# Attention with a relative bias, then a leaky-ReLU feed-forward: which banks the spare in-pieces take, how batch 0's v is split, and where the fifth pair's rows are copied

## The chip, the cores and the metric

The kernel runs on one core of a Trainium2 chip. The metric is the device time of one execution in microseconds. Five engines work side by side and meet at semaphores: TensorE (PE; its weight loads are shown apart as PEld), VectorE (DVE), ScalarE (ACT), GpSimd (POOL, which here mostly issues loads) and SyncE (SP, which issues stores and transposing DMAs). Matrix products are written to PSUM, in banks of 128 x 512 float32; a bank can be written again only when the engine that reads it is done.

## The reference, cut to what matters

```python
# q, k, v: (8, 8, 576, 64); bias_table: (32, 8); w_in: (512, 2048); w_out: (2048, 512)
scores = matmul(q, k.T) / sqrt(64) + bias_table[bucket(|i - j|)]   # per batch and head
attn = exp(scores - max) / sum(exp(scores - max))
x = matmul(attn, v)                     # to (4608, 512): 8 heads x 64 beside each other
h = x @ w_in
out = maximum(0.01 * h, h) @ w_out      # (4608, 512) float32
```

The bias depends on the distance alone and is constant from distance 128 on, so the kernel multiplies the exponentials by a band of factors near the diagonal and leaves the constant out, which the division cancels.

## The kernel before, in words

**Pairs.** Work goes by pairs of heads: 8 batches with 4 pairs each, n = 0 to 31. A sequence of 576 is cut into four chunks of 128 (NJ = 4) and a tail of 64. For a pair, the rows of q and k are copied beside each other (`pair_rows`, L263, two DVE copies), turned (`transpose_q`, `transpose_k`, L295 and L300; by PE and the m banks up to pair 8, by DMA after that) and multiplied. `score(n, u)` is one part of the scores and its exponential on ACT: u = 0 to 3 are the four key chunks against the first 512 queries (`ps_s`, two buffers of two banks, L320, exponential L333), u = 4 is the last 64 queries against the four chunks (written to the banks o0 and o1, one for each head, L313, exponential in two halves L336), u = 5 is the 64 tail keys (L323 and L324, in a `ps_s` buffer, exponential L340). `band(n, u)` multiplies an exponential by its band factors on DVE (L356).

**Value product.** `av_tails(n)` (L369) multiplies the 64 tail keys with the tails of v, for both heads, and `av(n, e)` (L380) the four chunks for head e; each head has its bank, o0 or o1. DVE then divides (reciprocal L383, product L384) into `opair`, which is transposed into xT by PE (L402, L403) or by DMA (L395).

**Feed-forward.** Rows of xT are taken in groups of 512. An in-piece (`ffn_in`, L428) is four products of 512 columns with w_in into one bank, followed by the leaky ReLU (`leaky`: ACT's Prelu at L439, or DVE at L436 and L437). An out-piece (`ffn_out`, L453) is four products with w_out; four of them fill one bank, which DVE copies out (L471). Both use the two m banks in turn (`bank`), unless `spare` names o0 or o1.

**The order** is written out by hand, engine by engine, in the code's order. From pair 5 on each pair has, in PE's order: scores 0 and 1, the tail products of the pair before, its value product for head 0, a slot with at most one in-piece, the product for head 1, a second slot, scores 2 to 4, then `moe_block` with score 5 inside it. `groups_of` shares out how many pieces a pair gets. If no out-piece is ready, the block does up to four in-pieces: the first two on m banks, the third on o0, the fourth on o1, the last two of them after score 5. Otherwise it does four out-pieces. At the end `moe(2, 0)` or `moe(2)` adds up to two in-pieces; in the first form the first of them sits on o0. The third in-piece of a block occurs in pairs 5, 6, 10, 11, 15 and 20, a fourth in pairs 10, 11, 15 and 20; a single piece at the end after four out-pieces in pairs 9, 13, 14, 17, 18 and 19, two in pairs 21 to 31. After pair 31, `moe_rest` does what is left of the feed-forward.

**The first four pairs** have no feed-forward beside them and an order of their own (L642 to L681). In the last of them, n = 3, `pair_rows(4)` comes first, so that in DVE's order its copies stand before bands 5 and 4 of pair 2, and `transpose_k(4)` comes before score 2.

**Loads** are issued by POOL in order. Batch 0: q and k of heads 0 and 1, 2 and 3, 4 and 5; v of heads 0 and 1, one load each; the two tails of these two heads; q and k of heads 6 and 7; then v of heads 2 to 7 in four chunks and the two tails of these six heads. Then come batch 1 and the weights. POOL issues a load only when the eighth load before it has landed.

Of the kernel before, what the change touches and what calls it, by code (L numbers as in the profile page):

```python
# [37 lines left out]
def kernel(  # L38
# [10 lines left out]
    nc = tc.nc  # L49

    B, H, S, D = q.shape
# [4 lines left out]
    P = 128  # L56
    n_pairs = H // 2
    NJ = S // P
    SL = S - NJ * P
# [34 lines left out]
    NBUF = 2  # L94
# [4 lines left out]
    vn = [per.tile([P, NJ, H, D + 1], BF16, name=f"vn{i}") for i in range(NBUF)]  # L99
    v4 = [per.tile([P, n_pairs, D + 1], BF16, name=f"v4_{i}") for i in range(NBUF)]  # L100
# [13 lines left out]
                in_=src[b, h0:h1, :, :].rearrange("h (r c) d -> r h (c d)", c=NC),  # L114
            )

    def load_v_part(b, chunks, tail):
        i = b % NBUF
        for c in chunks:
            nc.gpsimd.dma_start(  # L120
                out=vn[i][:, c, :, 0:D],
                in_=v[b, :, c * P : (c + 1) * P, :].rearrange("h s d -> s h d"),
            )
        if tail:
            for e in range(2):
                nc.gpsimd.dma_start(
                    out=v4[i][e * SL : (e + 1) * SL, :, 0:D],
                    in_=v[b, e::2, NJ * P : S, :].rearrange("h s d -> s h d"),
                )

    def load_v(b, h0, h1, by_head):
        i = b % NBUF
        p0, p1 = h0 // 2, h1 // 2
        if by_head:
            for h in range(h0, h1):
                nc.gpsimd.dma_start(
                    out=vn[i][:, :, h, 0:D],
                    in_=v[b, h, 0 : NJ * P, :].rearrange("(c s) d -> s c d", s=P),
                )
        else:  # L140
            for c in range(NJ):
                nc.gpsimd.dma_start(  # L142
                    out=vn[i][:, c, h0:h1, 0:D],
                    in_=v[b, h0:h1, c * P : (c + 1) * P, :].rearrange("h s d -> s h d"),
                )
        for e in range(2):
            nc.gpsimd.dma_start(
                out=v4[i][e * SL : (e + 1) * SL, p0:p1, 0:D],
                in_=v[b, h0 + e : h1 : 2, NJ * P : S, :].rearrange("h s d -> s h d"),
            )  # L150

    def clear_v(eng, i):
# [41 lines left out]
    for j, (u, lo, w, m) in enumerate(groups):  # L194
        copy = nc.scalar.copy if j % 3 == 2 else nc.vector.tensor_copy
        copy(out=ub[:, C0 + lo : C0 + lo + m * w].rearrange("h (m w) -> h m w", w=w),
             in_=e8[:, u : u + m].unsqueeze(2).to_broadcast([H, m, w]))
    row = ub[:, :]
    nc.vector.tensor_copy(
        out=ub[:, C0 - BAND + 1 : C0],  # L200
# [33 lines left out]
    load_qk(0, 2, 4)  # L234
    load_qk(0, 4, 6)
    clear_edges(nc.vector, 1)
    load_v(0, 0, 2, True)
    load_qk(0, 6, H)
    load_v(0, 2, H, False)
    clear_v(nc.gpsimd, 1)  # L240
    load_qk(1, 0, H // 2)
    load_qk(1, H // 2, H)
# [20 lines left out]
    def pair_rows(n):  # L263

        b, p = items[n]
        t = prs[n] = pr_pool.tile([RQ, 2, NC, 2 * D], BF16, name="pr")
        for j, src in enumerate((qn, kn)):
            nc.vector.tensor_copy(out=t[:, j, :, :].rearrange("r c (e d) -> r c e d", e=2),
                                  in_=src[b % NBUF][0:RQ, 2 * p : 2 * p + 2, :, :].rearrange("r e c d -> r c e d"))
# [25 lines left out]
    def transpose_q(n):  # L295
        qt = qts[n] = qt_pool.tile([P, S], BF16, name="qt")
        copy = nc.scalar.copy if n <= n_pairs else nc.vector.tensor_copy
        copy(out=qt[:, 0:S].rearrange("p (r c) -> p r c", c=NC), in_=turned_pair(n, 0))  # L298

    def transpose_k(n):  # L300
        kt = kts[n] = kts_[n % 2]
        nc.vector.tensor_copy(out=kt[:, 0:S].rearrange("p (r c) -> p r c", c=NC), in_=turned_pair(n, 1))  # L302
        apart(kt)
# [38 lines left out]
    def band(n, u):  # L342
        b, p = items[n]
        at, at4 = at_view(n), at4_[n % 2]
        hp = hk[:, 2 * p : 2 * p + 2, :]
        if u == 0:
            o, m = at[:, :, 0, 0 : 2 * P], mirrored(hp, P, 3 * P)
        elif u in (1, 2):
            o, m = at[:, :, u, (u - 1) * P : (u + 2) * P], mirrored(hp, 0, 3 * P)
        elif u == NJ:  # L350
            o, m = at[:, :, 3, 2 * P : S], mirrored(hp, 0, S - 2 * P)
        elif u == NJ + 1:
            o, m = at4[:, 3 * P : S], mirrored(hk4[:, p, :], 0, P + SL)
        else:
            return
        nc.vector.tensor_tensor(out=o, in0=o, in1=m, op=ALU.mult)  # L356
# [62 lines left out]
    def ffn_in(T, f, spare=None):  # L419
        if f == 0:  # L420
            gts[T] = gt_pool.tile([P, n_fc, TT], BF16, name="gt")
        t0 = T * TT
        if spare is None:
            pm = bank("pm1")
        else:
            pm = ps_o_pool.tile([P, 512], FP32, name="pm1", tag=f"o{spare}")
        for c in range(n_cc):
            nc.tensor.matmul(pm, lhsT=w_in_sb[:, c, f * P : (f + 1) * P], rhs=xT[c][:, t0 : t0 + TT],  # L428
                             start=(c == 0), stop=(c == n_cc - 1))
        return pm  # L430

    def leaky(T, f, pm, by_vector=False):
        g = gts[T][:, f, :]
        if by_vector:
            low = low_pool.tile([P, TT], BF16, name="low")
            nc.vector.tensor_scalar(low, pm, 0.01, None, op0=ALU.mult)  # L436
            nc.vector.tensor_tensor(out=g, in0=low, in1=pm, op=ALU.max)  # L437
        else:
            nc.scalar.activation(g, pm, AF.Prelu, bias=0.0, scale=1.0, alpha=0.01)  # L439
# [72 lines left out]
    def moe(n_pieces, spare=None):  # L512
        for _ in range(n_pieces):
            if room["left"] > 0 and can("in"):
                piece_in(spare)
                spare = None
                room["left"] -= 1
# [26 lines left out]
    def moe_block():  # L544

        done = 0
        while not can("out") and can("in") and done < 4 and room["left"] > 0:
            T, f = step("in")
            leaky(T, f, ffn_in(T, f, done - 2 if done > 1 else None), done == 1)
            room["left"] -= 1  # L550
            done += 1
            if done < 3:
                yield
        while done < 2:
            done += 1
            yield
        if can("out") and room["left"] >= 4:
            for part in range(4):
                piece_out()
                room["left"] -= 1  # L560
                if part == 1:
                    yield
            moe(2, 0)
        else:
            yield
            moe(2)
        yield
# [30 lines left out]
    def loads(n):  # L598

        b, p = items[n]  # L600
        if n == 0:
            load_w_in(0)
            load_v(1, 0, H, False)
            load_w_in(1)
            load_w_out(0)
        elif n == 2:
            load_qk(2, 0, H // 2)
            load_w_out(1)
        if b < 1 or p < 1 or b > B - 2:
            return  # L610
        nc.gpsimd.tensor_copy(out=tick, in_=ops_[n - 2][0:1, 0, 0:1])  # L611
        if p == 1:
            load_qk(b + 1, H // 2, H)
            load_v_part(b + 1, (0,), False)
        elif p == 2:
            load_v_part(b + 1, (1, 2, 3), False)
        else:
            load_v_part(b + 1, (), True)
            if b + 2 < B:
                load_qk(b + 2, 0, H // 2)  # L620

    def begin(n):
        loads(n)
        if n_pairs < n + 1 < N and not by_dma(n + 1):
            pair_rows(n + 1)
        for m in range(n + 2, min(n + AHEAD + 1, N)):
            if by_dma(m) and m - (AHEAD if m > 2 * n_pairs + 2 else 2) == n:
                pair_rows(m)
                turn_by_dma(m)

    def score(n, u):
        exp(n, u, qk_mm(n, u))
# [7 lines left out]
    score(0, 0)  # L640
    score(0, 1)
    for n in range(n_pairs):  # L642
        begin(n)
        if n == n_pairs - 1:
            pair_rows(n + 1)
        if n > 1:
            band(n - 1, 5)
            band(n - 1, 4)
        if n == 1:
            for u in (0, 1, 2, 5, 4):  # L650
                band(0, u)
        if n == 0:
            score(n, 2)
        transpose_k(n + 1)
        if n < 2:
            spin(3)
        if n > 0:
            score(n, 2)
        if n == 1:
            score(n, 3)  # L660
        if n > 0:
            av_tails(n - 1)
            av(n - 1, 0)
            band(n, 0)
        if n != 1:
            score(n, 3)
        if n > 0:
            av(n - 1, 1)
        transpose_q(n + 1)
        if n < 1:  # L670
            spin(3)
        score(n, 5)
        if n > 0:
            band(n, 1)
            x_transposes(n - 1)
            band(n, 2)
        if n < n_pairs - 2:
            pair_rows(n + 2)
        score(n, 4)
        score(n + 1, 0)  # L680
        score(n + 1, 1)  # L681
# [106 lines left out]
```

## Time and profile before

| | before |
|---|---|
| median of 3 runs (lowest, highest) | 388.04 us (386.69, 388.61) |
| profiled execution | 389.03 us |
| its span, first to last instruction | 387.2 us |
| PE busy | 368.6 us (95%) |
| ACT busy | 241.9 us (62%) |
| DVE busy | 205.0 us (53%) |
| POOL busy | 76.5 us (20%) |
| mean granted TensorE clock | 0.996 |

The profile is of one execution. Busy time is the time in which an engine has an instruction under way; matrix products are pipelined and their ends are modelled. In the rows of the timeline the columns are: start, duration, engine, line, operation, what it writes and reads, how many instructions are merged, and in brackets the idle time of the engine ahead of it with what ended it. In the table of waits they are: who waited for what, the sum in us, how many times, the longest. A row of a window gives its length and for PE, PEld, DVE, ACT and POOL the busy time, then the granted TensorE clock, the share of the DMA engines and GB/s. Times are us from the start of the span.

### The profile page before, as it was taken

The numbers are of one execution on the slowest core, as the hardware profiler recorded it, in microseconds if no ns is written. First come the engines' busy times: TensorE is split into PE (matmuls) and PEld (weight loads), VectorE is DVE, ScalarE is ACT, GpSimd is POOL, SyncE is SP. The second block draws the span as 40 slices with busy tenths as digits, with TensorE's granted clock in tenths as the row PEclk, the third lists the DMA queues.
The fourth block names the chain that finished last, engine by engine and source line by source line (L and its number), as shares of the span: only waits on it lengthen the run. The fifth ranks groups of instructions, "written<-read, shape, count | busy, mean of one in ns | idle before, by whom it ended". The sixth has DMA issues, their size and how long they took to land.

```text
span 387.2 us, 8539 instructions
## 1 busy us (share of the span) xinstructions
PE 368.6 (95%) x3501; PEld 187.3 (48%) x3501; DVE 205.0 (53%) x520; ACT 241.9 (62%) x376; POOL 76.5 (20%) x118
## 2 busy tenths in 40 slices
PE   7878988999999999999999999999999999999996
PEld 3445554555444444544455555555555544444442
DVE  5778577776666666666665666655554300110221
ACT  4979678476857768777687777777777546045000
POOL 8764320223023303330323032100000000000000
PEclk9989999999999999999999999999999999999999
DMA  9999999899849983998699859933211100110122
GB/s 106 180 204 184 207 187 120 99 182 126 109 63 163 126 134 54 162 115 133 106 116 105 130 90 132 129 73 71 40 44 46 46 27 0 56 54 0 59 80 81
DMA packets 104351, 40.05 MB, mean 103 GB/s; under 512 B 83184, under 2 KB 98808, under 8 KB 104312
## 3 DMA queue, kind: packets, MB, share of 16 engines
q0 software_dynamic: 53696, 18.36, 46.0%
q1 hardware_dynamic: 50472, 21.02, 27.1%
q8 instruction: 27, 0.44, 0.5%
q10 hardware_dynamic: 144, 0.13, 0.1%
q14 instruction: 12, 0.10, 0.1%
HBM read 37.68 MB, written 9.45 MB: 122 GB/s over the span
## 4 chain that ended last, share of the span: by engine, by line
PE 80%; DVE 6%; ACT 5%; DMA 4%; POOL 3%; issue 1%; DVEq 0%; POOLq 0%
PE pm L453 31%; PE pm L428 28%; PE ps_o L380 9%; PE ps_s L320 6%; ACT at L333 3%; DMA v<-in_v_dram 2%; ACT gt L439 2%; DVE at L356 2%; DMA xT<-opair 2%; DVE opair L384 2%; PE ps_o L369 2%; PE ps_s L323 1%; DVE qt L298 1%; POOL vn L142 1%; PE ps_tx L402 1%
## 5 line engine op out<-in xcount | busy, mean ns | idle before, releaser
L428 PE MATMUL pm<-xT,w_in_sb 128*128 128x512 bf16 x576 | 138.2, 379 | 5.0 <-ACT at L336 4.6
L439 ACT ACTIVATE gt<-pm 128x512 bf16<-128x512 f32 x138 | 82.7, 599 | 92.5 <-PE pm L428 91.9
L453 PE MATMUL pm<-w_out_sb,gt 128*128 128x512 bf16 x576 | 132.5, 379 | 0.0
L333 ACT ACTIVATE at<-ps_s 128x1024 bf16<-128x1024 f32 x128 | 124.7, 1028 | 8.9 <-PE ps_s L320 8.9
L356 DVE TENSOR_TENSOR at<-at,hk 128x768 bf16<-128x768 bf16 (+3 forms) x160 | 71.4, 453 | 31.5 <-ACT at L336 20.8
L453 PEld LDWEIGHTS <-gt 128*128 128x128 bf16 x576 | 53.0, 98 | 60.6
L428 PEld LDWEIGHTS <-w_in_sb 128*128 128x128 bf16 x576 | 52.4, 98 | 59.4 <-issue 5.4
L471 DVE COPY y<-pm 128x512 f32<-128x512 f32 x33 | 22.8, 691 | 76.7 <-PE pm L453 76.7
L380 PE MATMUL ps_o<-vn,at 128*128 128x65 bf16 x1280 | 50.4, 195 | 0.0
L380 PEld LDWEIGHTS <-at 128*128 128x128 bf16 x1280 | 45.3, 98 | 9.3 <-issue 1.4
L320 PE MATMUL ps_s<-qt,kt 64*128 64x512 bf16 x256 | 40.2, 383 | 1.9 <-ACT at L333 1.4
L383 DVE RECIPROCAL rcp<-ps_o 128x5 f32<-128x5 f32 x64 | 12.3, 192 | 53.4 <-PE ps_o L380 53.4
L611 POOL COPY tick<-opair 1x1 bf16<-1x1 bf16 x18 | 4.6, 255 | 156.6 <-DVE opair L384 156.6
L384 DVE TENSOR_TENSOR opair<-ps_o,rcp 128x320 bf16<-128x320 f32 x64 | 31.5, 492 | 3.3
L120 POOL DMA_DIRECT2D vn<-in_v_dram x24 | 22.8, 956 | 2.6 <-issue 1.1
L340 ACT ACTIVATE at<-ps_s 128x576 bf16<-128x576 f32 x32 | 21.9, 685 | 1.2 <-PE ps_s L324 1.2
L336 ACT ACTIVATE at<-ps_q 128x256 bf16<-128x256 f32 x64 | 21.6, 405 | 0.4 <-PE ps_q L313 0.3
L320 PEld LDWEIGHTS <-kt 64*128 64x128 bf16 x256 | 8.2, 94 | 27.7 <-issue 20.7
L463 ACT COPY y<-pm 128x256 f32<-128x256 f32 x1 | 0.4, 372 | 27.5 <-DVE y L463 27.5
L369 PEld LDWEIGHTS <-at 64*128 64x128 bf16 x320 | 9.4, 94 | 12.3 <-issue 5.7
L302 DVE COPY kt<-tu 128x576 bf16<-128x576 bf16 x23 | 15.3, 664 | 0.0
L298 DVE COPY qt<-tu 128x576 bf16<-128x576 bf16 x23 | 15.0, 650 | 0.0
(57 smaller groups left out, 195.3 us busy)
## 6 DMA issues: line engine op xcount, KB each, us to landing
out_dram<-y SPq DMA_DIRECT2D x35, 256.0 KB, 2.3
qn<-in_q_dram POOLq DMA_DIRECT2D x14, 288.0 KB, 5.0
kn<-in_k_dram POOLq DMA_DIRECT2D x14, 288.0 KB, 6.1
vn<-in_v_dram POOLq DMA_DIRECT2D x28, 128.0 KB, 5.7
w_in_sb<-in_moe_w_in_dram POOLq DMA_DIRECT2D x2, 1024.0 KB, 12.8
w_out_sb<-in_moe_w_out_dram POOLq DMA_DIRECT2D x2, 1024.0 KB, 16.0
qn<-in_q_dram POOLq DMA_DIRECT2D x4, 144.0 KB, 4.1
kn<-in_k_dram POOLq DMA_DIRECT2D x4, 144.0 KB, 4.2
```

Source lines behind the costliest of these rows:

```text
L120: nc.gpsimd.dma_start(out=vn[i][:, c, :, 0:D], in_=v[b, :, c * P : (c + 1) * P, :].rearrange("h s d -> s h d"),)
L320: nc.tensor.matmul(ps[:, e, :], lhsT=kt[r, u * P : (u + 1) * P], rhs=qt[r, 0:512], start=True, stop=True)
L333: nc.scalar.activation(at[:, :, u, 0:512], ps, AF.Exp, scale=scale)
L336: nc.scalar.activation(at[:, e, :, 512:S], ps[e][:, 0 : NJ * SL].rearrange("p (c i) -> p c i", i=SL), AF.Exp, scale=scale)
L340: nc.scalar.activation(at4[:, 0:S], ps.rearrange("p e i -> p (e i)")[:, 0:S], AF.Exp, scale=scale)
L356: nc.vector.tensor_tensor(out=o, in0=o, in1=m, op=ALU.mult)
L380: nc.tensor.matmul(ps[:, ic, :], lhsT=at[:, o : o + P], rhs=vn[b % NBUF][:, c, 2 * p + e, :], start=False, stop=(ic == NJ and c == NJ - 1))
L384: nc.vector.tensor_tensor(out=opair[:, :, e * D : (e + 1) * D], in0=ps[:, :, 0:D], in1=rcp.to_broadcast([P, NJ + 1, D]), op=ALU.mult)
L428: nc.tensor.matmul(pm, lhsT=w_in_sb[:, c, f * P : (f + 1) * P], rhs=xT[c][:, t0 : t0 + TT], start=(c == 0), stop=(c == n_cc - 1))
L439: nc.scalar.activation(g, pm, AF.Prelu, bias=0.0, scale=1.0, alpha=0.01)
L453: nc.tensor.matmul(pm, lhsT=gt[:, f, ts * P : (ts + 1) * P], rhs=w_out_sb[:, f, :], start=(f == 0), stop=(f == n_fc - 1))
L471: nc.vector.tensor_copy(out=y, in_=pm)
```

## The change

Three things are changed.

1. Of the in-pieces that follow score 5 in a block, only the fourth keeps its bank of the value product (o1); the third takes the next m bank. At a pair's end after out-pieces the first piece sits on o0 only if more than one piece is left to do.
2. Batch 0's v: the tails of all eight heads are loaded where those of heads 0 and 1 were; heads 2 and 3 are then loaded by head, and heads 4 to 7 by chunk. The other batches' loads are the same, by functions that are cut in another way.
3. In the fourth pair (n = 3) the rows of the fifth are copied after the first value product of pair 2 and a band, `transpose_k(4)` moves behind the second value product, and score 5 moves ahead of both transposes.

```diff
-    def load_v_part(b, chunks, tail):
...
-    def load_v(b, h0, h1, by_head):
...
+    def load_v_part(b, chunks, h0=0, h1=H):
         for c in chunks:
             nc.gpsimd.dma_start(
+                out=vn[b % NBUF][:, c, h0:h1, 0:D],
+                in_=v[b, h0:h1, c * P : (c + 1) * P, :].rearrange("h s d -> s h d"),
             )
+    def load_v_head(b, h):
+        nc.gpsimd.dma_start(
+            out=vn[b % NBUF][:, :, h, 0:D],
+            in_=v[b, h, 0 : NJ * P, :].rearrange("(c s) d -> s c d", s=P),
+        )
+    def load_v_tail(b):
         for e in range(2):
             nc.gpsimd.dma_start(
+                out=v4[b % NBUF][e * SL : (e + 1) * SL, :, 0:D],
+                in_=v[b, e::2, NJ * P : S, :].rearrange("h s d -> s h d"),
             )
...
-    load_v(0, 0, 2, True)
+    load_v_head(0, 0)
+    load_v_head(0, 1)
+    load_v_tail(0)
     load_qk(0, 6, H)
-    load_v(0, 2, H, False)
+    load_v_head(0, 2)
+    load_v_head(0, 3)
+    load_v_part(0, range(NJ), 4, H)
...
-            leaky(T, f, ffn_in(T, f, done - 2 if done > 1 else None), done == 1)
+            leaky(T, f, ffn_in(T, f, 1 if done == 3 else None), done == 1)
...
-            moe(2, 0)
+            moe(2, 0 if room["left"] > 1 else None)
...
     for n in range(n_pairs):
+        last = n == n_pairs - 1
         begin(n)
-        if n == n_pairs - 1:
-            pair_rows(n + 1)
...
-        transpose_k(n + 1)
+        if not last:
+            transpose_k(n + 1)
...
             av_tails(n - 1)
             av(n - 1, 0)
             band(n, 0)
+        if last:
+            pair_rows(n + 1)
         if n != 1:
             score(n, 3)
         if n > 0:
             av(n - 1, 1)
+        if last:
+            score(n, 5)
+            transpose_k(n + 1)
         transpose_q(n + 1)
         if n < 1:
             spin(3)
-        score(n, 5)
+        if not last:
+            score(n, 5)
```

More of the change, by code (lines that the diff above doesn't have):

```diff
@@ L115, in load_qk @@
             )
-    def load_v_part(b, chunks, tail):
-        i = b % NBUF
+    def load_v_part(b, chunks, h0=0, h1=H):
         for c in chunks:
             nc.gpsimd.dma_start(
-                out=vn[i][:, c, :, 0:D],
-                in_=v[b, :, c * P : (c + 1) * P, :].rearrange("h s d -> s h d"),
-            )
[L124 to L129, printed above, removed]
-    def load_v(b, h0, h1, by_head):
[L132 to L145, printed above, removed]
+                out=vn[b % NBUF][:, c, h0:h1, 0:D],
+                in_=v[b, h0:h1, c * P : (c + 1) * P, :].rearrange("h s d -> s h d"),
+            )
+    def load_v_head(b, h):
[4 more added lines that the diff above has]
+    def load_v_tail(b):
         for e in range(2):
             nc.gpsimd.dma_start(
-                out=v4[i][e * SL : (e + 1) * SL, p0:p1, 0:D],
-                in_=v[b, h0 + e : h1 : 2, NJ * P : S, :].rearrange("h s d -> s h d"),
+                out=v4[b % NBUF][e * SL : (e + 1) * SL, :, 0:D],
+                in_=v[b, e::2, NJ * P : S, :].rearrange("h s d -> s h d"),
             )
@@ L602, in loads @@
             load_w_in(0)
-            load_v(1, 0, H, False)
+            load_v_part(1, range(NJ))
+            load_v_tail(1)
             load_w_in(1)
@@ L613, in loads @@
             load_qk(b + 1, H // 2, H)
-            load_v_part(b + 1, (0,), False)
+            load_v_part(b + 1, (0,))
         elif p == 2:
-            load_v_part(b + 1, (1, 2, 3), False)
+            load_v_part(b + 1, (1, 2, 3))
         else:
-            load_v_part(b + 1, (), True)
+            load_v_tail(b + 1)
             if b + 2 < B:
```

## The prediction

> **What bounds the kernel now.** I read the page first (span, clock line, costliest groups), then the waits of PE, then the timeline around each long wait. The page:
>
> ```profile
> span 387.2 us, 8539 instructions
> PE 368.6 (95%) x3501; PEld 187.3 (48%) x3501; DVE 205.0 (53%) x520; ACT 241.9 (62%) x376; POOL 76.5 (20%) x118
> PE 80%; DVE 6%; ACT 5%; DMA 4%; POOL 3%; issue 1%; DVEq 0%; POOLq 0%
> ```
>
> TensorE is busy 95% of the span and carries 80% of the chain, so a wait of PE that goes shortens the span, unless PE soon meets another wait. The time to be had is the 387.2 - 368.6 = 18.6 us that PE idles. The waits of PE (whole span; the last row: weight loads from 36 to 200 us) show where:
>
> ```profile
> PE pm L428 <- ACT at L336: 4.6, 6, 0.8
> PE ps_o L369 <- DMA v<-in_v_dram: 0.8, 1, 0.8
> ...
> PEld L369 <- issue: 3.9, 9, 0.4
> ```
>
> The first row is the third in-piece of a block, which sits on bank o0 and waits for the exponential of part 4 to read that bank; the second is the tail of v; the last is the first tail product of a pair, nine times. The three edits aim at these rows.
>
> **The change part by part.** The order of instructions on each engine is the same but for the fifth pair's rows, transposes and copies, and batch 0's v loads; no instruction is added or dropped, and SP's queue is unchanged. Which bank a piece writes is not an instruction: it changes waits only. By the code's rules the third in-piece occurs in pairs 5, 6, 10, 11, 15, 20 (six, as the first row has), and a lone piece at a pair's end in pairs 9, 13, 14, 17, 18, 19.
>
> *Third in-piece, four-piece blocks (pairs 10, 11, 15, 20).* Timeline of PE and of ACT in pair 10:
>
> ```profile
> 96.92 0.19 PE L324 MATMUL ps_s<-qt,kt 128*128 128x64 bf16 x1
> 97.88 2.75 PE L428 MATMUL pm<-xT,w_in_sb 128*128 128x512 bf16 x12 [0.77 <-ACT at L336]
> 100.56 0.60 PE L320 MATMUL ps_s<-qt,kt 64*128 64x512 bf16 x4
> 101.01 0.31 PE L369 MATMUL ps_o<-v,at 64*128 64x65 bf16 x10
> ...
> 96.04 0.60 ACT L439 ACTIVATE gt<-pm 128x512 bf16<-128x512 f32 x1
> 97.44 0.67 ACT L336 ACTIVATE at<-ps_q 128x256 bf16<-128x256 f32 x2
> ```
>
> On an m bank the third piece takes the buffer of the first piece of the block, which ACT left at 96.04 + 0.60 = 96.64, so it starts when PE is free, about 97.0. A piece takes about 0.87 us (three in 97.88 to 100.5), so it ends at 97.85. The fourth piece stays on o1, which the second half of L336 leaves at 97.44 + 0.67 = 98.11; it starts at 98.17 instead of 97.88 + 0.87 = 98.75. Gain 0.58 a pair, not 0.77: 0.3 us of wait stays on o1. Four pairs: 2.3 us. In pair 11, where the fourth piece is the last, the next tail product still waits for o1, as now.
>
> *Pairs 5 and 6 (third piece alone).* Pair 5:
>
> ```profile
> 51.04 0.19 PE L324 MATMUL ps_s<-qt,kt 128*128 128x64 bf16 x1
> 52.00 1.02 PE L428 MATMUL pm<-xT,w_in_sb 128*128 128x512 bf16 x4 [0.77 <-ACT at L336]
> 52.95 0.61 PE L320 MATMUL ps_s<-qt,kt 64*128 64x512 bf16 x4
> 53.71 0.33 PE L369 MATMUL ps_o<-v,at 64*128 64x65 bf16 x10
> ...
> 52.08 0.69 ACT L340 ACTIVATE at<-ps_s 128x576 bf16<-128x576 f32 x1
> 53.06 0.60 ACT L439 ACTIVATE gt<-pm 128x512 bf16<-128x512 f32 x1 [0.29 <-PE pm L428]
> ```
>
> The piece would end at 51.95. Next late is the second score of the next pair: its bank is free when L340 ends, at 52.77. So it starts at 52.83, and the tail products at 53.05 instead of 53.71; they no longer wait for the Prelu that reads o0 until 53.66. Gain 0.66 each, 1.3 us.
>
> *Lone piece at the end (six pairs).* Pair 9 into 10, PE, then ACT and DVE:
>
> ```profile
> 90.25 0.60 PE L320 MATMUL ps_s<-qt,kt 64*128 64x512 bf16 x4
> 91.01 0.33 PE L369 MATMUL ps_o<-v,at 64*128 64x65 bf16 x10
> 91.88 1.03 PE L428 MATMUL pm<-xT,w_in_sb 128*128 128x512 bf16 x4
> ...
> 90.36 0.60 ACT L439 ACTIVATE gt<-pm 128x512 bf16<-128x512 f32 x1 [1.80 <-PE pm L428]
> ...
> 89.50 0.69 DVE L471 COPY y<-pm 128x512 f32<-128x512 f32 x1 [0.65 <-PE pm L453]
> ```
>
> From the scores to the tail products there are 0.76 us here and 0.45 in pair 10 (100.56 to 101.01), where no piece holds o0: 0.31 us lost to the Prelu that ends at 90.96. On m it goes: 6 x 0.31 = 1.9 us. The price is an added wait: the next slot's piece (91.88) now takes the buffer of the output piece, which the copy L471 leaves at 90.19. It would come at 91.57, so 1.4 us of cover remain; cost nothing, and behind it would stand the rest of PE's pair.
>
> These three sum to 2.3 + 1.3 + 1.9 = 5.5 us; I take 5.4, since pair 11's last wait may grow by 0.1. Bounds: 1.9 (only the Prelu waits go), and 6 x 0.77 + 8 x 0.31 = 7.1 (every wait goes whole).
>
> *Batch 0's v.* The whole tail goes out ahead of q and k of heads 6 and 7, and heads 2 and 3 ahead of the rest. PE and ACT in the third pair, POOL's queue, and PE, DVE, ACT, POOL and the granted clock by stretches of 3.4 us:
>
> ```profile
> 21.85 0.56 PE L369 MATMUL ps_o<-v,at 64*128 64x65 bf16 x10 [0.84 <-DMA v<-in_v_dram]
> 24.04 1.02 ACT L333 ACTIVATE at<-ps_s 128x1024 bf16<-128x1024 f32 x1 [1.67 <-PE ps_s L320]
> 25.79 0.64 ACT L298 COPY qt<-ps_t 128x576 bf16<-128x576 bf16 x1 [0.72 <-PE ps_t L284]
> 18.66 0.67 POOL L112 DMA_DIRECT2D kn<-in_k_dram  x1 [0.67 <-DMA vn<-in_v_dram]
> 19.20:22.60 3.40, 1.60 (x28) 0.93 (x27) 2.51 (x8) 3.17 (x5) 1.41 (x3) 1.00 1.44 192
> 22.60:26.00 3.40, 3.40 (x48) 2.52 (x44) 1.73 (x6) 1.23 (x2) 3.40 (x5) 0.50 1.29 207
> 26.00:29.40 3.40, 2.46 (x47) 1.50 (x46) 3.32 (x8) 3.40 (x7) 1.59 (x3) 1.00 1.13 213
> ```
>
> Ten loads before, ten after, the same bytes. By the shapes in the code a head is 64 KB, both of its pair's tails 16 KB, a chunk of six heads 96 KB. Up to the second chunk, for whose landing POOL waited until 18.66, 128 + 16 + 192 = 336 KB of v were issued; in the changed order 128 + 64 + 128 = 320 KB hold all that the second pair needs. So it is there before 21.85 - 0.84 = 21.01, where PE began to wait. The larger tails move q and k of heads 6 and 7 by 48 KB, half a chunk; DVE first uses them for the fourth pair. With the stall the half clock behind it goes, if nothing else brings it (a rival, below). ACT gets back 1.67 + 0.72 = 2.4 us; it then runs without a gap and sets the pace. I take 2.2 (bounds 0.8, the DMA wait alone, and 2.4).
>
> *Fifth pair's rows.* DVE, PE, and ACT in the fourth pair:
>
> ```profile
> 27.36 0.35 DVE L268 COPY pr<-qn 96x768 bf16<-96x768 bf16 x1
> 27.63 0.57 DVE L268 COPY pr<-kn 96x768 bf16<-96x768 bf16 x1
> 28.73 0.76 DVE L302 COPY kt<-ps_t 128x576 bf16<-128x576 bf16 x1
> 29.52 0.23 DVE L290 TENSOR_TENSOR kt<-kt,own 128x128 bf16<-128x128 bf16 x1
> 33.63 0.65 DVE L356 TENSOR_TENSOR at<-at,hk 128x192 bf16<-128x192 bf16 x2
> 28.26 0.43 PE L284 MATMUL ps_t<-ident,pr 96*128 96x96 bf16 x6 [0.83 <-DVE pr L268]
> 29.10 0.78 PE L380 MATMUL ps_o<-vn,at 128*128 128x65 bf16 x20
> 33.93 0.24 PE L369 MATMUL ps_o<-v,at 64*128 64x65 bf16 x4 [0.47 <-DVE at L356]
> 27.40 3.87 ACT L333 ACTIVATE at<-ps_s 128x1024 bf16<-128x1024 f32 x4
> ```
>
> Today rows, kt copy and mask fill DVE from 27.36 to 29.75, before the pair's first division. Moved behind that division and a band, they put 0.57 + 0.76 + 0.23 = 1.6 us (the two row copies overlap) into a stretch in which DVE hardly idles, up to the bands of 33.63 that PE awaits at 33.93. In return the first division comes only 0.2 earlier: PE's 0.83 wait for the rows goes, but the third score then waits for a bank until the first exponential ends, 27.40 + 3.87 / 4 = 28.4. The 0.2, and about as much by which each copy starts before the one ahead has quite ended, come off: cost 1.2 (bounds 0 and 1.6). Behind the bands stand the rest of pair 3's products, its transposes and the first in-pieces. The first scores of pair 4 need kt too, which now comes after the second division, so ACT may idle some tenths before them; that lies inside the 1.2, since the products wait longer.
>
> Sum: 5.4 + 2.2 - 1.2 = 6.4 us off. The profiled execution took 389.03 us (387.2 of span and 1.8 around it), the median of the runs is 388.04; I count from 388.5, between them: **382.1 us**.
>
> **The rivals.**
> *The half clock comes back.* The clock is 0.50 from 22.60 to 26.00, after 3.4 us in which PE was busy 1.60; after 2.46 busy it stayed at 1.00. In the changed fourth pair PE idles some 1.3 us until the first exponential frees a bank, and idles twice shortly before, so a stretch of 3.4 us can again be about half busy. Then both value products of pair 2 run slow; one took
>
> ```profile
> 22.34 1.12 PE L380 MATMUL ps_o<-vn,at 128*128 128x65 bf16 x20
> ```
>
> against 0.78 at 29.10: 2 x 0.34 and, with the scores between, about 0.9 us given back: 383.0 us. The Trainium skill, TensorE: Matmul & The Clock Gate, Part 1, says that a free-running window of about 3.4 us with too little PE activity halves the clock; the 3.4 us of 0.50 here agree. By that rule the window's place in each run decides.
>
> *The rows cost more than v gives.* If v brings only its DMA wait of 0.8 and the rows cost 1.6 with 0.4 of ACT behind kt, the early part loses 1.2: 388.5 - 5.4 + 1.2 = 384.3 us.
> *The third piece's wait only moves.* If the fourth piece on o1, or L340's bank, takes back all the 0.77, eight Prelu waits remain as gain: 388.5 - 8 x 0.31 - 1.0 = 385.0 us. The end of L336 speaks against it (0.67 for both halves).
> *Slower.* At the six lone pieces the next slot now waits for the output copy L471. Suppose that copy comes behind the next pair's first division: the product for it ends near 91.88 - 0.31 = 91.57; with the division estimated at the copy's own length, 0.69 each, the buffer is free at 92.95, 1.4 us late, and DVE's rows in between (0.35 + 0.57) make it 2.3: 6 x 2.3 = 13.8, 395.9 us. It decides from 1.4 us a pair (8.3 / 6, to 390.4). The row at 89.50 speaks against it: the copy starts there as soon as the output piece is done.
>
> **How the numbers follow.** Forecast 0.49 (its own range 380.8 to 383.5), half clock 0.23, rows 0.09, moved wait 0.11, slower 0.08. About 0.5% (1.9 us: 386.1 to 390.0) is what a measurement of this kernel can tell from no change. Faster: 0.49 + 0.23 + 0.09 and 0.07 of the moved wait = 0.88; within: 0.04 of it and 0.02 of the last = 0.06; slower 0.06. The range 380.3 to 385.4 takes in the first three and half the fourth; below it lie only both best bounds.
>
> **What would show it.** Right: the wait of L428 for L336 falls from 4.6 to about 1.2 (four times 0.3); the L369 issue waits fall from nine to about one; no wait for v near 21; the fourth pair's bands and the tail products behind them later relative to its start. Wrong: L428 waiting for a DVE copy or a Prelu in the slots, 0.50 clock between 25 and 30 us, or pair 4 starting no earlier than now.

## The result, and the profile after

The changed kernel took 383.54 us (median of 6 runs, 382.98 to 384.84) against 387.28 us for the kernel before (median of 6, 386.69 to 388.61): 0.990 of the time, 95% interval 0.988 to 0.992. The profiled execution took 383.14 us, with a span of 381.4.

From the page of the changed kernel (its line numbers are lower: L428 became L417, L380 became L369, L369 became L358):

```profile
span 381.4 us, 8484 instructions
PE 363.4 (95%) x3447; PEld 186.9 (49%) x3501; DVE 205.0 (54%) x520; ACT 240.7 (63%) x376; POOL 76.0 (20%) x118
PE 83%; DVE 7%; ACT 6%; issue 2%; another core or an unknown queue 1%; DVEq 0%; ACTq 0%
L417 PE MATMUL pm<-xT,w_in_sb 128*128 128x512 bf16 x544 | 136.5, 379 | 2.6 <-ACT at L325 0.7
```

TensorE is still the bound. The waits of PE over the whole span:

```profile
PE ps_s L309 <- ACT at L322: 2.7, 3, 1.2
...
PE ps_s L309 <- ACT at L329: 1.0, 3, 0.4
...
PE pm L417 <- ACT at L325: 0.7, 4, 0.2
PE ps_o L358 <- DVE at L345: 0.4, 1, 0.4
```

The wait of the third piece for the exponential of part 4 was 4.6 us in six waits; 0.7 in four is left, on the fourth piece. The DMA wait for v is gone. At the top now are scores that wait for an exponential: 2.7 us where it was 1.4, of which 1.23 are one wait in the fourth pair.

PE in pairs 5, 9 and 10 of the changed kernel:

```profile
51.22 1.03 PE L417 MATMUL pm<-xT,w_in_sb 128*128 128x512 bf16 x4
52.97 0.39 PE L309 MATMUL ps_s<-qt,kt 64*128 64x512 bf16 x2 [0.40 <-ACT at L329]
53.19 0.33 PE L358 MATMUL ps_o<-v,at 64*128 64x65 bf16 x10
...
89.06 0.61 PE L309 MATMUL ps_s<-qt,kt 64*128 64x512 bf16 x4
89.50 0.32 PE L358 MATMUL ps_o<-v,at 64*128 64x65 bf16 x10
...
95.43 1.03 PE L417 MATMUL pm<-xT,w_in_sb 128*128 128x512 bf16 x4
96.64 1.89 PE L417 MATMUL pm<-xT,w_in_sb 128*128 128x512 bf16 x8 [0.18 <-ACT at L325]
```

In pair 5 the piece starts behind score 5, and the second score then waits 0.40 for L329 (before L340). In pair 9 the tail products follow 0.44 behind the scores, where it was 0.76. In pair 10 the fourth piece waits 0.18 for the second half of the exponential.

To see where the time goes, take the start of the part-4 scores of each pair (L313 before, L302 after) and subtract the first trace of the kernel before. Each column is one trace, in us; pairs are numbered from 0, so that pair 2 is the third and pair 3 the fourth. The last three columns are runs told of below.

| pair | before, us | changed | banks alone | v and banks | before, the trace at full clock |
|---|---|---|---|---|---|
| 1 | 18.64 | -0.05 | 0.05 | 0.07 | 0.26 |
| 2 | 26.42 | -2.12 | 0.57 | -2.11 | -1.83 |
| 3 | 32.12 | -1.09 | 0.61 | -2.30 | -1.97 |
| 4 | 38.67 | 0.16 | 0.84 | -2.33 | -1.99 |
| 6 | 58.20 | -0.51 | 0.17 | -2.99 | -1.98 |
| 12 | 115.90 | -2.69 | -2.01 | -5.17 | -2.00 |
| 13 | 124.48 | -3.06 | -2.38 | -5.54 | -1.97 |
| 21 | 200.46 | -5.86 | -5.18 | -8.33 | -1.97 |
| 31 | 299.70 | -5.86 | -5.18 | -8.33 | -1.97 |

The changed kernel gains 2.12 us up to pair 2, gives back 1.03 by pair 3 and 1.25 by pair 4, and then gains 6.0 us up to pair 21; nothing changes after that. PE and DVE in its third to fifth pair, and two stretches of 3.4 us:

```profile
21.04 0.32 PE L358 MATMUL ps_o<-v,at 64*128 64x65 bf16 x10
26.31 0.39 PE L309 MATMUL ps_s<-qt,kt 64*128 64x512 bf16 x2 [1.23 <-ACT at L322]
28.57 0.35 DVE L257 COPY pr<-qn 96x768 bf16<-96x768 bf16 x1
29.25 0.68 PE L273 MATMUL ps_t<-ident,pr 96*128 96x96 bf16 x12 [0.40 <-DVE pr L257]
30.66 0.44 PE L391 MATMUL ps_tx<-ident,opair 128*128 128x128 bf16 x5 [0.73 <-ACT qt L287]
32.51 0.65 DVE L345 TENSOR_TENSOR at<-at,hk 128x192 bf16<-128x192 bf16 x2
32.82 0.29 PE L358 MATMUL ps_o<-v,at 64*128 64x65 bf16 x4 [0.45 <-DVE at L345]
33.05 1.28 PE L369 MATMUL ps_o<-vn,at 128*128 128x65 bf16 x20
29.40:32.80 3.40, 2.06 (x35) 1.28 (x33) 3.37 (x10) 2.22 (x5) 0.56 (x1) 0.98 2.15 161
32.80:36.20 3.40, 3.38 (x48) 2.58 (x48) 1.13 (x4) 2.13 (x3) 1.70 (x3) 0.52 1.75 179
```

The tail products no longer wait for v. The last bands begin 1.1 us earlier than in the first trace (32.51 against 33.63), not 2.1. Then, from about 32.7 to 36.1, the clock is halved: the value product takes 1.28 instead of 0.78. All that v had given in this trace is gone by pair 4.

### The profile page after: what moved, and what is told of

Its sections match the earlier page's. It is cut to its first block, busy times and chain, and to the rows that moved or that the text cites. A ratio compares the mean times of both kernels' runs of the same rounds, so it can differ in the third digit from the quotient of the medians.

```text
span 381.4 us, 8484 instructions
## 1 busy us (share of the span) xinstructions
PE 363.4 (95%) x3447; PEld 186.9 (49%) x3501; DVE 205.0 (54%) x520; ACT 240.7 (63%) x376; POOL 76.0 (20%) x118
## 4 chain that ended last, share of the span: by engine, by line
PE 83%; DVE 7%; ACT 6%; issue 2%; another core or an unknown queue 1%; DVEq 0%; ACTq 0%
PE pm L442 32%; PE pm L417 28%; PE ps_o L369 10%; PE ps_s L309 7%; ACT at L322 4%; DVE at L345 2%; DVE opair L373 2%; PE ps_w L579 1%; PE ps_o L358 1%; PE ps_s L312 1%; ACT at L325 1%; PE ps_tx L391 1%; DVE qt L287 1%; DVE pr L257 1%
## 5 line engine op out<-in xcount | busy, mean ns | idle before, releaser
L417 PE MATMUL pm<-xT,w_in_sb 128*128 128x512 bf16 x544 | 136.5, 379 | 2.6 <-ACT at L325 0.7
L428 ACT ACTIVATE gt<-pm 128x512 bf16<-128x512 f32 x138 | 83.0, 602 | 88.1 <-PE pm L417 86.9
L442 PE MATMUL pm<-w_out_sb,gt 128*128 128x512 bf16 x555 | 130.8, 379 | 1.1
L417 PEld LDWEIGHTS <-w_in_sb 128*128 128x128 bf16 x576 | 52.1, 98 | 55.5 <-issue 2.0
L369 PE MATMUL ps_o<-vn,at 128*128 128x65 bf16 x1280 | 50.6, 195 | 0.0
L369 PEld LDWEIGHTS <-at 128*128 128x128 bf16 x1280 | 45.4, 99 | 9.0 <-issue 0.9
L119 POOL DMA_DIRECT2D vn<-in_v_dram x32 | 28.8, 909 | 2.7 <-issue 1.1
L329 ACT ACTIVATE at<-ps_s 128x576 bf16<-128x576 f32 x32 | 21.8, 682 | 1.2 <-PE ps_s L313 1.2
L112 POOL DMA_DIRECT2D qn<-in_q_dram x18 | 13.9, 773 | 2.4 <-DMA vn<-in_v_dram 1.0
```

The source lines that it names most:

```text
L119: nc.gpsimd.dma_start(out=vn[b % NBUF][:, c, h0:h1, 0:D], in_=v[b, h0:h1, c * P : (c + 1) * P, :].rearrange("h s d -> s h d"),)
L329: nc.scalar.activation(at4[:, 0:S], ps.rearrange("p e i -> p (e i)")[:, 0:S], AF.Exp, scale=scale)
L369: nc.tensor.matmul(ps[:, ic, :], lhsT=at[:, o : o + P], rhs=vn[b % NBUF][:, c, 2 * p + e, :], start=False, stop=(ic == NJ and c == NJ - 1))
L442: nc.tensor.matmul(pm, lhsT=gt[:, f, ts * P : (ts + 1) * P], rhs=w_out_sb[:, f, :], start=(f == 0), stop=(f == n_fc - 1))
```

## The experiments

Each was timed beside the kernel before on one chip. The mean granted clock of an execution tells whether a stretch of half clock was in it: 3.4 us at 0.5 are 0.0045 of the span, so about 0.995 with one such stretch, 0.990 with two, and 0.998 or more with none or a part of one. "Full clock" below means 0.998 or more.

**The kernel before, unchanged, and once more for a trace.**

> The kernel before, unchanged, run several times to see what its executions differ by. Theory (the half clock behind the v stall comes and goes with the window's place): executions fall into two groups, one near 386.9 us with a mean granted clock near 1.000, one near 388.5 us with 0.996; the difference is about 1.5 us. Rival (every execution has the half clock once): all have 0.996 and differ by chance.

> The kernel before once more, for a trace. If the clock is 1.000 in it: theory A has PE wait for v about as in the first trace and yet the fourth or fifth pair some 2 us earlier, since the products behind the wait run at full clock; rival B has no wait for v at all in such an execution.

Measured: 387.74 us (386.66 to 390.19, 12 runs), ratio 1.000 (0.997 to 1.003). Six executions at full clock took 386.66 to 387.18 us, six with 0.990 or 0.996 took 388.30 to 390.19. So the kernel before splits into two groups 2.3 us apart in the median (386.90 and 389.21), more than the 1.5 expected. Over all executions of the kernel before in these experiments, 35 of 70 were at full clock. The second run, for its trace, took 387.03 us, at full clock. PE in its third pair, and two stretches:

```profile
20.74 0.43 PE L284 MATMUL ps_t<-ident,pr 96*128 96x96 bf16 x6 [1.12 <-DVE pr L268]
21.33 0.32 PE L369 MATMUL ps_o<-v,at 64*128 64x65 bf16 x10
19.20:22.60 3.40, 2.28 (x44) 1.34 (x40) 3.19 (x9) 3.37 (x5) 2.37 (x4) 1.00 1.35 198
22.60:26.00 3.40, 2.46 (x47) 1.59 (x45) 3.26 (x9) 3.27 (x7) 3.08 (x5) 1.00 1.27 208
```

Here v is in time. The tail products do not wait, and the third pair is 1.83 us earlier than in the first trace, with the same code. The rival was right for this trace: no wait at all.

One of the 12 executions (388.85 us, mean clock 0.990) also left a trace. PE in its third pair, and the stretches around it:

```profile
20.45 0.43 PE L284 MATMUL ps_t<-ident,pr 96*128 96x96 bf16 x6 [1.03 <-DVE pr L268]
21.61 0.66 PE L369 MATMUL ps_o<-v,at 64*128 64x65 bf16 x10 [0.28 <-DMA v<-in_v_dram]
19.20:22.60 3.40, 2.07 (x30) 1.16 (x27) 2.69 (x8) 3.23 (x5) 2.23 (x3) 0.76 1.44 189
22.60:26.00 3.40, 3.40 (x47) 2.54 (x44) 1.71 (x6) 1.21 (x2) 3.40 (x5) 0.50 1.29 206
26.00:29.40 3.40, 2.81 (x39) 1.53 (x38) 3.06 (x8) 3.22 (x6) 1.42 (x3) 0.74 1.13 213
```

A mean of 0.76 means half clock for 1.63 of the 3.4 us, so it sets in near 21.0; by the 0.74 it ends near 27.8. That is 6.8 us, two stretches in a row. PE begins to wait for v only at 21.61 - 0.28 = 21.33: here the clock was halved before v was late.

**The banks alone.**

```diff
-            leaky(T, f, ffn_in(T, f, done - 2 if done > 1 else None), done == 1)
+            leaky(T, f, ffn_in(T, f, 1 if done == 3 else None), done == 1)
...
-            moe(2, 0)
+            moe(2, 0 if room["left"] > 1 else None)
```

> Only the banks of the third in-piece and of the lone piece at a pair's end are changed; v and the fifth pair's rows as before. Theory: the whole gain of the changed kernel after pair 4, 6.0 us of span, is from here: by pair -0.66 in 5 and 6, -0.32 in six pairs, -0.58 in 10, 11, 15, 20, and the time about 381.3 us in the median. Rival (the early edits make room that the pieces use): clearly less than 5 us.

Measured: 382.10 us (381.15 to 384.05, 6 runs), ratio 0.986 (0.982 to 0.989). By pair the steps are those of the changed kernel: from pair 4 to pair 21 its offset falls by 0.84 + 5.18 = 6.0 us. One step, 0.37 between pairs 12 and 13, also shows in traces whose banks are as before (the unchanged kernel's, both early edits, the rows alone): it is the 0.2 us wait for the transposed x and what hangs on it, which comes and goes. Without it the banks give 5.65. At full clock the medians are 381.19 against 387.04 us on the same chip, 5.85 less.

**The early edits alone** (v's split and the rows), **and each by itself.** The diff of the first is the change without the two lines above; of the others, one part of it.

> Only v's split and the fifth pair's rows are changed; the pieces' banks as before. Theory: third pair 2.1 us earlier, fourth 1.1 earlier, then the half clock from about 33 to 36 us takes it back: 387 to 388.7 us, clock 0.995, no faster than the kernel before. Rival (the half clock in the changed kernel's profile was chance): about 1.1 us faster, 386 us, with clock near 1.000 in some executions.

> Only v's split is changed. Theory A (v's wait costs only through the half clock that may follow it; where that stays away the wait is made up within the next pairs): executions with clock 1.000 near the kernel before's undisturbed ones, 386.7 to 387.2 us, and the half clock gone or rarer, so the median about 1 us under the kernel before's. Rival B (v's wait costs 2.2 us in itself): near 384.8 us.

> Only the fifth pair's rows, transposes and score 5 are moved. Theory (they lengthen DVE's work behind the first division by 1.0 us): executions with clock 1.000 about 1 us longer than undisturbed ones of the kernel before, near 387.8 us, and others with the half clock near 389.5; the offset between the third and the fifth pair about +1.0 us. Rival (with v late the rows are hidden): no difference.

Measured: both, 388.96 us (12 runs), ratio 1.003 (1.001 to 1.005): 0.3% slower. v alone, 386.64 us (12 runs), ratio 0.999 (0.997 to 1.001): not told from no change, and far from the rival's 384.8. Rows alone, 389.50 us (12 runs), ratio 1.005 (1.003 to 1.007): 0.5% slower. At full clock, against the kernel before at full clock timed beside them, the medians are +1.16, -0.29 and +1.31 us. In the profile of both, at full clock throughout, the fourth pair still loses 1.0 us on the third, and the offset then stays: the loss is there without any half clock. v alone had 9 of 12 executions at full clock, the rows alone 2 of 12, both 4 of 12.

The rows alone leave v's loads as they were. Their trace is at full clock throughout, and v is late in it:

```profile
21.39 0.59 PE L369 MATMUL ps_o<-v,at 64*128 64x65 bf16 x10 [0.25 <-DMA v<-in_v_dram]
29.40:32.80 3.40, 2.09 (x36) 1.36 (x35) 3.33 (x10) 2.22 (x6) 0.89 (x1) 1.00 2.05 165
32.80:36.20 3.40, 2.88 (x59) 1.99 (x58) 2.36 (x9) 3.15 (x4) 1.53 (x3) 1.00 1.82 174
```

Up to the part-4 scores of pair 2 the two kernels have the same order, so this trace can be set beside the one with mean clock 0.990 above: v is late by 0.25 and 0.28 us, and the scores start at 24.93 and 26.70. The 1.77 us between them come with the half clock, not with the wait for v.

**v and the banks, the rows in their old place.** Against the changed kernel:

```diff
     for n in range(n_pairs):
-        last = n == n_pairs - 1
         begin(n)
+        if n == n_pairs - 1:
+            pair_rows(n + 1)
...
-        if not last:
-            transpose_k(n + 1)
+        transpose_k(n + 1)
...
-        if last:
-            pair_rows(n + 1)
...
-        if last:
-            score(n, 5)
-            transpose_k(n + 1)
         transpose_q(n + 1)
...
-        if not last:
-            score(n, 5)
+        score(n, 5)
```

> The changed kernel with the fifth pair's rows, transposes and score 5 in their old places: v's split and the banks alone. Theory (moving the rows costs 1.0 us on DVE and the idle PE behind it brings the half clock, 1.25 us): 2.2 us shorter than the changed kernel, about 381.2 us, clock near 1.000, the fourth pair 2.1 us earlier than in the kernel before. Rival (the rows had to move, since the earlier fourth pair waits for batch 1's rows to land or stalls score 2): no faster than the changed kernel, 383.5 us or more, with a wait of DVE or PE for the rows near 25 us.

> v's split and the banks with the rows in their old place, beside the changed kernel on one chip. Theory: about 381.1 us, 0.6% under the changed kernel, clock at 0.998 or more in nearly all executions. Rival (chips differ by as much): no difference beyond 0.3%.

> The changed kernel again, to see on one chip beside the version without the moved rows how often the half clock comes. Theory (the moved rows bring it in nearly every execution): clock 0.996 or less in most executions, about 383.5 us, and near 382 us where the clock is 1.000. Rival (it was chance): half of them at 1.000, as in the kernel before.

Measured: 381.13 us (380.57 to 381.93, 6 runs), ratio 0.983 (0.979 to 0.986); beside the changed kernel on one chip 381.12 (5 runs), ratio 0.982 (0.979 to 0.984), against 383.38 (381.97 to 385.51, 6 runs), ratio 0.988 (0.985 to 0.992), for the changed kernel. All 11 executions were at full clock. This version is the best here, 2.3 us under the changed kernel. PE in its fourth and fifth pair:

```profile
25.93 0.43 PE L273 MATMUL ps_t<-ident,pr 96*128 96x96 bf16 x6 [0.84 <-DVE pr L257]
31.60 0.24 PE L358 MATMUL ps_o<-v,at 64*128 64x65 bf16 x4 [0.45 <-DVE at L345]
31.77 0.78 PE L369 MATMUL ps_o<-vn,at 128*128 128x65 bf16 x20
29.40:32.80 3.40, 2.80 (x49) 1.69 (x49) 2.66 (x8) 3.25 (x6) 0.85 (x1) 1.00 2.05 166
```

PE does wait 0.84 us for the rows, as before the change, and yet the tail products come at 31.60 instead of 32.82: the wait is shorter than what the moved rows cost later. DVE copies these rows without a wait, so batch 1's loads had landed in time and the rival's stall is not there. Of the changed kernel's 12 executions, two were at full clock (382.05 in the median); ten were not. One of the two left a trace: there the offset of the table goes from -2.03 at pair 2 to -1.01 at pair 3 and -1.03 at pair 4. So the moved rows cost 1.0 us without any half clock, and the 1.25 us lost by pair 4 in the profile above are the half clock's. With the runs of both early edits and of the rows alone, kernels with the moved rows were at full clock in 8 of 36 executions, kernels with v's split and the rows in their old place in 20 of 23.

**PE kept at work in the fourth pair.** Against the changed kernel; the first call stands at the start of the fourth pair, the second behind `transpose_q`:

```diff
+    def spin_s(k):
+        pw = ps_s_pool.tile([P, 2, 512], FP32, name="ps_s")
+        for _ in range(k):
+            nc.tensor.matmul(pw[:, 0, :], lhsT=junk[:, 0:P], rhs=junk, start=True, stop=True)
...
+        if last:
+            spin(4)
...
+        if last:
+            spin_s(3)
```

> The changed kernel with seven products of zeros added on PE in the fourth pair: four at its start, three behind the transposes, both where PE idles; their results are used by nothing. Theory (the idle PE behind the moved rows brings the half clock): clock 1.000 in nearly all executions, the pairs from 4 on about 1.2 us earlier than in the changed kernel's profile, about 382 us. Rival (the half clock comes whatever PE does there, or the added products cost as much): 383.5 us or more.

Measured: 382.42 us (381.71 to 382.94, 6 runs), ratio 0.987 (0.984 to 0.990), all at full clock. The added products and the stretches around them:

```profile
24.93 1.02 PE L579 MATMUL ps_w<-junk 128*128 128x512 bf16 x3
29.57 0.81 PE L584 MATMUL ps_s<-junk 128*128 128x512 bf16 x2
32.78 0.78 PE L369 MATMUL ps_o<-vn,at 128*128 128x65 bf16 x20
29.40:32.80 3.40, 2.64 (x38) 1.40 (x37) 3.37 (x10) 2.23 (x5) 0.69 (x1) 1.00 2.10 165
32.80:36.20 3.40, 3.25 (x62) 2.33 (x59) 2.32 (x7) 2.95 (x3) 1.56 (x3) 1.00 1.88 182
```

DVE and ACT do the same in 29.4 to 32.8 as in the changed kernel (3.37 and 2.2 us busy), PE 2.64 instead of 2.06, and the product takes 0.78. By the starts of the part-4 scores the fourth pair still loses 1.03 us on the third, as in the changed kernel's profile, and the fifth loses 0.03 instead of 1.25; so what these products bring is the clock. On the same chip the rows alone were at full clock in 2 of 12 executions, so it is not the chip. The executions are near 382, where the changed kernel's two at full clock are; the cost of the moved rows stays.

## Why the prediction was right or wrong

The time, 383.54 us, lies in the range, and the kernel is faster, but the likeliest case was not the one that came: 382.1 was forecast without the half clock; the first rival, the half clock, gave 383.0 and is what the trace shows. That the time is within 1.4 us of the forecast is in part luck. The forecast took 6.4 us off; against the kernel before timed beside it, 387.28 us, the change took off 3.7. The base of 388.5 was 1.2 us too high, and that hides nearly half of the difference. One of the signs of being wrong came true: pair 4 starts no earlier than before (0.16 us later in the table).

*Third in-piece.* Right in place and size. Forecast 0.58 a pair in four pairs, with 0.3 us of wait left on o1: the steps are 0.58 to 0.59 and the wait left is 0.18. Forecast 0.66 in pairs 5 and 6, with the second score held by L340's bank: 0.66 and 0.68, and the row shows that wait, 0.40.

*Lone piece.* Right: 0.31 forecast, 0.32 to 0.33 measured in six pairs; no slot waits for the output copy. Between 36 and 200 us, where the first tail product of a pair was held up nine times, one time is left:

```profile
PEld L358 <- issue: 0.4, 1, 0.4
```

With pair 11's allowance the pieces were put at 5.4; they give 5.65.

*Batch 0's v.* Here the forecast failed, in its size and in the step "with the stall the half clock behind it goes". "I take 2.2" was read from one execution, and in the trace of the changed kernel the third pair is indeed 2.12 us earlier. But half of the executions of the kernel before are at full clock, and the trace of one of those shows v landing in time; among such executions v's split alone gives 0.29 us, and its interval does not tell it from nothing. So the term was worth 2.2 only against an execution that had the half clock. And the half clock does not hang on the stall: in one trace it sets in ahead of the wait for v, in another v is late and the clock stays at 1.00. The profiled execution of the kernel before took 389.03 us, longer than each of the 6 timed runs; the base of 388.5 leaned on it.

*Fifth pair's rows.* Right: cost 1.2 forecast, 1.0 by the offsets between pairs 2 and 3, with and without half clock, and 1.3 in the medians at full clock. DVE carries the copies behind the first division, and PE's wait for them only gave way to a wait for the first exponential, 1.23 us.

*The half clock.* Given 0.23 and 0.9 us; it came in 10 of 12 executions and took 1.25 us in the trace, up to 2.1 in the medians (382.05 and 384.15 on one chip; some of these executions have it twice). The rival had its sign right, a stretch with much idle time on PE (2.06 of 3.4 us busy), but the place was off by a stretch: it fell not on pair 2's products but on pair 3's, after 29.4 to 32.8, where PE waits for the moved rows (0.40), for the copy of the turned q (0.73) and for the late bands (0.45). That more work on PE there keeps the clock up is shown by the added products: 6 of 6 executions at full clock, 2 of 12 without them. Why half the executions of the kernel before have the half clock is not settled. With v's split and the rows in their old place it is rarer (20 of 23 at full clock against 35 of 70), but how the order of v's loads does that, and what makes v late in some executions, was not tried.

The parts add up at full clock: -5.85 for the banks, -0.29 for v and +1.31 for the rows make -4.8 us; the changed kernel's two executions at full clock are 5.1 under those of the kernel before on that chip (382.05 and 387.14). The forecast's 6.4 differs from this mainly by its 2.2 for v.

## What to carry to other kernels

A piece that borrows a bank from another stage inherits that stage's reader as its wait, and hands its own reader on as a wait to the next; count both ends. Read a stall in a profile as a term of a sum only after seeing whether other executions have it: the spread of the times and the mean granted clock tell. Removing a wait by moving its cause to a place where the engine is full can cost more than the wait, here 1.0 to 1.3 us for 0.8.

## What the runs showed of the hardware that was not expected

The half clock needs no long idle time. The longest single wait of PE in the 3.4 us ahead of it was 0.90 us in the first trace and 0.73 us in the changed kernel. The Trainium skill, TensorE: Matmul & The Clock Gate, HAM oscillation, gives as the abstract rule that PE must not idle for more than about 3.4 us; that would have let both pass, and the measurement decides.

The busy time of PE in such a stretch does not decide it alone either. The half clock came after 1.60 us of 3.4 in the first trace and after 2.06 in the changed kernel. But with the rows alone 2.09 was followed by full clock (the rows above), and so were 2.03 with the banks alone and 2.14 in the changed kernel's trace at full clock, from which these two rows are:

```profile
26.00:29.40 3.40, 2.03 (x29) 1.01 (x28) 3.28 (x10) 3.22 (x6) 1.88 (x3) 1.00 1.13 213
29.40:32.80 3.40, 2.14 (x35) 1.36 (x35) 3.35 (x10) 2.22 (x5) 0.59 (x1) 1.00 2.10 164
```

These stretches are cut at the same times in every trace, and the half clock is not. Four traces have it before the end of the kernel. In their record of the granted clock the first entry at full clock begins at 3.87 to 5.51 us; the half clock sets in 17.07 us after that in three of them and 27.31 us in the fourth, five and eight times 3.41, and lasts 3.41 us, in one trace twice that. So its steps lie on a grid of 3.41 us, which lies differently in each execution. Cut by this grid, the stretches ahead of the half clock had PE busy for 1.37, 1.62, 1.73 and 2.21 us; in other traces stretches with 1.85 (the kernel before), 1.98 (both early edits) and 2.20 (the rows alone) were not followed by it. What decides besides PE's busy time stays open. The same page of the Trainium skill, Part 1, has a free-running window of about 3.4 us; it agrees with the length of the half clock here, 22.6 to 26.0 and 32.7 to 36.1, and with a kernel that has it in some executions and not in others.
